# An FNet-gated kernel on one core: earlier draining of four accumulators, one sum taken by an accumulating transfer, and about forty transfers issued by GpSimd instead of SyncE

## The chip, the cores and the metric

One core of a Trainium2 chip runs the whole program. The metric is the device time in microseconds of one execution, the median over several runs. Five engines take part: TensorE (PE in the profile, with its weight loads as PEld), VectorE (DVE), ScalarE (ACT), GpSimd (POOL) and SyncE (SP). SP computes nothing here; it issues transfers. GpSimd computes nothing here either but for a few constants at the start; it too issues transfers.

## What is computed

With S = 2048 tokens and D = 512 features, F = 1792:

```
xn = layernorm(x)
a, b = xn @ Wd_re.T, xn @ Wd_im.T
s = Ws_re @ a - Ws_im @ b                  # FNet mixing, real part
h = relu(xn @ w1 + b1) ** 2
g = silu(h @ w2 + b2)
out = x + s * g
```

Everything is float32.

## The kernel before

A float32 operand is split into a rounded high part (HI, a ScalarE copy, line 138) and the remainder (LO, a VectorE subtraction, line 141). A product then takes three passes on TensorE: HI·HI, HI·LO, LO·HI. Big products are done on 2x2 blocks with seven block products instead of eight, so that operands are needed not only as they are but also as sums of their blocks.

The sequence transform comes first. The tokens lie in eight "x pairs" j (block j and block j + 8, 128 tokens each), the matrix of the transform in eight chunks c of 256 columns. `XC[j]` (tiles `xc`) holds the split operands of pair j, `u` the raw block (c, j) of the transform's matrix with its sums behind it (four quarters raw, four quarters sums), `g` the split form of that. The work comes in this order:

1. A loop over j = 0..7 loads x, normalizes it, splits it and does chunk 0 with plain products (`products`, line 406) into four PSUM banks `accs`.
2. Two steps `plain_step(j)` for j = 4 and 5 (`MIXED`) do chunk 1 of these pairs with eight plain products, 48 matmuls each (line 395). They need neither the sums of x nor those of the matrix.
3. The list `steps`: first (1, 0), (1, 1), (1, 2), (1, 3), (1, 6), (1, 7), then (c, j) for c = 2 to 7. Each step n does seven products of 6 matmuls, 42 in all (line 395), behind a pipeline written out by hand: in iteration n the block of step n + 4 is loaded (`step_load`), the sums of step n + 2 are made (`step_sums`) and step n + 1 is split (`step_split`). The end of a chunk goes out to DRAM as P and Q (`PQD`). In between, `EARLY` makes the second-stage weights: load (`weight`, line 445), sums, split, store to DRAM (line 458), and loads of the stored ones (`load_wd`, line 509).
4. The hidden transform (Y units), the first dense layer (H units) and the second with the gate and the output follow.

What the change touches lies at the seam of 1, 2 and 3:

- `sums(g)` makes the sums of x for four pairs (g = 0: pairs 0 to 3, g = 1: pairs 4 to 7) as a generator: three VectorE subtractions (line 275), one at each `next`, and then four accumulating transfers that GpSimd issues (line 278), 128 KB each, one for each pair. `split_sums(j)` splits what comes out: HI on ScalarE, LO on VectorE.
- `sums_b` makes the four sums of a block of the matrix with three VectorE operations: line 305 writes quarters 4 and 5 (quarter 0 plus quarters 1 and 2), lines 307 and 308 write quarters 6 and 7 out of these.
- `plain_out(k)` copies the four banks of chunk 0 to SBUF on ScalarE (line 148, tiles `plain`), whence SP stores them (line 628).

Each engine carries out its instructions in the order in which the program issues them; a wait of one holds all behind it. Transfers are queued by the engine that issues them. In this kernel SP issues nearly all loads and stores, ScalarE the stores of y and h, and GpSimd the eight accumulating transfers of the sums of x and seven accumulating additions of x near the end (line 945).

Of the kernel before, what the change touches and what calls it, by code (L numbers as in the profile page):

```python
# [8 lines left out]
F32 = mybir.dt.float32  # L9
F32R = mybir.dt.float32r  # L10
AF = mybir.ActivationFunctionType
ALU = mybir.AluOpType

P = 128
S, D, F = 2048, 512, 1792
NS, ND, NF = S // P, D // P, F // P
# [116 lines left out]
def fnet_gated_kernel(ctx, tc, x, xt, ct, wd, w1, w2, b1, b2, out):  # L133
    nc = tc.nc
# [8 lines left out]
    def split(*parts):  # L143
        split_hi(*parts)
        split_lo(*parts)
# [15 lines left out]
    PQD = [dram.tile([P, 2, 4, 256], F32, name=f"pqd{c}") for c in range(NC)]  # L161
    WDD = [dram.tile([P, 2, 7, 256], F32, name=f"wdd{n}") for n in range(ND)]
# [9 lines left out]
    def buf(tag, shape, name, dtype=F32):  # L172
        return pool.tile(shape, dtype, tag=tag, bufs=3 if tag == "u" else 1, name=name)
# [96 lines left out]
    def sums(g):  # L270


        s = xn32[ND * g, "tile"].rearrange("p j h (b n) -> p j (h b) n", b=2)
        for to, a, b in ((3, 1, 3), (1, 1, 0), (0, 3, 0)):
            nc.vector.tensor_tensor(s[:, :, to], s[:, :, a], s[:, :, b], op=ALU.subtract)
            yield
        for j in (1, 0, 3, 2):
            nc.gpsimd.dma_start(s[:, j, 2], s[:, j, 0], accum_op=ALU.add)
        yield

    def split_sums(j):
        s = xn32[j].rearrange("p h (b n) -> p (h b) n", b=2)
        split(XC[j][:, S2:S1 + 1, HI, :], XC[j][:, S2:S1 + 1, LO, :], s)

    raw, part = {}, {}

    def load_c(c, j, hs=slice(0, 2)):
        if (c, j) not in raw:
            raw[c, j] = buf("u", [P, 8, CW], f"u{c}_{j}")
        q = slice(2 * hs.start, 2 * hs.stop)  # L290
        nc.sync.dma_start(raw[c, j][:, q], ct[c, j, :, q])
# [8 lines left out]
    def sums_b(t, r):  # L300
        list(sums_b_steps(t, r))

    def sums_b_steps(t, r):

        nc.vector.tensor_tensor(t[:, 0:2], r[:, 0:1].to_broadcast([P, 2, 256]), r[:, 1:3], op=ALU.add)  # L305
        yield
        nc.vector.tensor_tensor(t[:, 2], t[:, 1], r[:, 1], op=ALU.add)  # L307
        nc.vector.tensor_tensor(t[:, 3], t[:, 2], r[:, 3], op=ALU.add)

# [32 lines left out]
    def step_sums(n):  # L342
        if n < len(steps):
            u = raw[steps[n]]
            sums_b(u[:, 4:8], u)

    def step_split(n):
        if n < len(steps):
            s = steps[n]
            u = raw.pop(s)  # L350
            g = part[s] = buf("g" + "ab"[s[1] % 2], [P, 2, 7, CW], f"g{s[0]}_{s[1]}", F32R)
            split(g[:, HI], g[:, LO], u[:, 1:8])
# [75 lines left out]
    steps = [(1, j) for j in SEVEN] + [(c, j) for c in range(2, NC) for j in range(NJ)]  # L428
    order = [(0, j) for j in range(NJ)] + [(1, j) for j in MIXED] + steps
# [12 lines left out]
    def weight(n, raw_, sums_, to, k, turn=False):  # L442

        r = buf("pq00", [P, 4, 256], f"{n}r")
        nc.sync.dma_start(r, raw_)
        yield
        t = buf("pq01", [P, 4, 256], f"{n}t")
        if turn:
            copy(r[:, I22:I21 + 1], r[:, I22:I21 + 1], -1.0)
        first = sums_(t, r)  # L450
        next(first)
        yield
        list(first)
        yield
        g = buf(f"wd{int(k)}", [P, 2, 7, 256], f"{n}g", F32R)
        for q, src in ((slice(0, 3), r[:, 1:4]), (slice(3, 7), t)):
            split(g[:, HI, q], g[:, LO, q], src)
            nc.sync.dma_start(to[:, :, q], g[:, :, q].bitcast(F32))
            yield

    makers["d"] = lambda n: weight(f"wd{n}", wd[n], sums_b_steps, WDD[n], n % 2, True)
# [43 lines left out]
    def load_wd(n):  # L505
        t = operand_buf(("wd0", "wd1", "xc2", "xc1")[n], f"wdp{n}", 0)
        WDP[n] = t
        for i in range(2):
            nc.sync.dma_start(t[:, i].bitcast(F32), WDD[n][:, i])
            yield  # L510

    makers["y"] = y_early
# [42 lines left out]
    g = plain_parts(0, 1)  # L555
# [3 lines left out]
    def some(steps_, n):  # L559
        for _ in range(n):  # L560
            next(steps_)

    side = sums(0), sums(1)
    load_c(0, 3)
    load_x(4)
    for j in range(1, NJ):
        ln_rstd(j)
        if j == 1:
            ln_hi(j, 0)
            ln_shift(j)  # L570
            ln_xn_act(j, 0)
            ln_mean(j + 1, 1)
            split_lo(*plain_parts(0, j, one))
            ln_xn(j, 1)
            split_hi(*xc_parts(j, 1))
            split_lo(*xc_parts(j, 0))
            split_lo(*plain_parts(0, j, two))
        else:
            if j == NJ - 1:
                ln_shift(j)  # L580
                next(side[0])
            for h in range(2):
                (ln_xn_act if j == NJ - 1 else ln_xn)(j, h)
                split_hi(*xc_parts(j, h))
            split_lo(*g)
            split_lo(*xc_parts(j, 0))
        load_c(*order[j + 3])
        if j in (1, 3, 4):
            load_x({1: 5, 3: 6, 4: 7}[j])
        if j + 1 < NJ:  # L590
            ln_stats(j + 1)
            if j > 1:
                ln_mean(j + 1, 1)
            ln_var(j + 1, 1)
            ln_root(j + 1)
        split_lo(*xc_parts(j, 1))
        if j == NJ - 1:
            some(side[0], 3)
        for h in range(2):
            products(j, h)  # L600
        g = plain_parts(*order[j + 1])
        split_hi(*g)
        if j == 2:
            nc.sync.dma_start(b1s, b1)
            nc.sync.dma_start(b2s, bcast(b2, D))
    split_lo(*g)
    some(side[1], 1)
    step_sums(0)


# [3 lines left out]
    def plain_out(k):  # L614
        to = plain[k // 2].rearrange("p (i m d t) -> p d m i t", i=2, m=2, d=2)[:, k % 2]
        copy(to, accs[k].rearrange("p (m i t) -> p m i t", m=2, i=2))

    for i, j in enumerate(MIXED):
        if i == 0:
            some(side[1], 1)  # L620
            split(*plain_parts(1, MIXED[1]))
            step_sums(1)
            for k in (0, 1):
                split_sums(k)
                plain_out(2 * k)
                plain_out(2 * k + 1)
            for k in range(2):
                nc.sync.dma_start(PQD[0][:, k].rearrange("p k n -> p (k n)"), plain[k])
        else:
            some(side[1], 2)  # L630
            step_split(0)
            split_sums(2)
        plain_step(j)
        load_c(*order[NJ + i + 4])
# [3 lines left out]
    for n, s in enumerate(steps):  # L638
        c, j = s
        if c > 1 and j == 0:  # L640
            ms = {}
        for k, tag in banks(c).items():
            if k not in ms:
                ms[k] = bank(tag, f"m{k}_{c}")
        g = part.pop(s)
        for p in FIRST if j == 0 and c > 1 else ORDER:
            a, b = PRODUCTS[p]
            mm(ms[p], XC[j][:, a], lambda b_: g[:, b_, b], (c > 1 and j == 0) or (not n and p in (1, 5, 6, 7)), s in LAST)
        step_sums(n + 2)
        step_split(n + 1)  # L650
        if n in SUMS_AT:
            split_sums(SUMS_AT[n])
        if n == 0:
            e = buf("e", [P, 2048], "c1")
            copy(chunk_part(e)(C22), halves(ms[Z]))
        step_load(n + 4)
        if closing:
            some(closing, (LATER_1 if c == 2 else LATER).get(j, 0))
            if j in (3, 4):
                q = slice((j - 3) * 1024, (j - 2) * 1024)  # L660
                nc.sync.dma_start(PQD[c - 1][:, j - 3].rearrange("p k n -> p (k n)"), e[:, q])
            if j == 4:
                closing = None
        if s in LAST:
            if c > 1:
                e = buf("e", [P, 2048], f"c{c}")
            room = {}
            if c < NC - 1:
                room = buf("pq10", [P, 2, 512], f"left{c}")
                room = {7: room[:, 0], 5: room[:, 1], 3: buf("pq11", [P, 512], f"left3_{c}")}  # L670
            closing = closing_of(chunk_part(e), ms, room, c == 1)
            some(closing, 2)
        if s == (2, 4):
            nc.vector.transpose(stats_t, stats.rearrange("p m h j -> p (m h j)"))
            for q in range(4):
                nc.sync.dma_start(rows[:, q * 32:(q + 1) * 32], stats_t[q * 32:(q + 1) * 32, :])
        go(*EARLY.get(s, ()))
# [326 lines left out]
    for u in range(2, NC):  # L1004
        n = 2 * u + 2
# [83 lines left out]
    for n in range(NTC * NP):  # L1089
        c, p = divmod(n, NP)  # L1090
# [37 lines left out]
        if p == NP - 1 and not last:  # L1128
            e = buf("e", [P, 4, 512], f"z{c}")
# [16 lines left out]
    e = buf("u", [P, 4, 512], f"z{c}")  # L1146
# [95 lines left out]
```

## Time and profile before

| | |
|---|---|
| median of three runs | 671.6 us (670.96 to 672.92) |
| the profiled execution's own time | 671.6 us |
| its span, first to last instruction | 669.7 us |
| granted TensorE clock, mean | 0.999 |
| PE busy | 662.0 us, 99% |
| DVE busy | 609.6 us, 91% |
| ACT busy | 384.2 us, 57% |
| POOL busy (transfers issued) | 15.9 us, 2% |
| transfers of q1 (issued by SP) | 129.28 MB, 57.9% of 16 DMA engines |
| transfers of q0 (issued by GpSimd) | 2.88 MB, 3.0% |

The profiled execution's time is 1.9 us above its span, and equal to the median of the runs, so that microseconds of the trace can be added to that median. PE is idle for 669.7 - 662.0 = 7.7 us in all. In rows of the trace a name like `g`, `u` or `xc` stands for all tiles of that name, so neighbours in time have to be told apart by their place in the order of the program.

### The profile page before, as it was taken

How to read it: one execution, taken by the hardware profiler on the slowest of the kernel's cores; microseconds unless marked ns; L12 is line 12 of the kernel's file. 1: busy time of each engine (PE TensorE's matmuls, PEld its weight loads, DVE VectorE, ACT ScalarE, POOL GpSimd, SP SyncE). 2: the span in 40 equal slices, each digit the busy share in tenths (PEclk: the TensorE clock that was granted, in tenths of full speed). 3: DMA queues.
4: the chain of work that ended last, by engine and by line, in shares of the span. 5: the costliest groups of instructions: out<-in, count | busy, mean ns of one | idle time of the engine just before them, and what ended most of it. 6: DMA issues, size and time to landing. Idle time of an engine off the chain costs nothing.

```text
span 669.7 us, 13552 instructions
## 1 busy us (share of the span) xinstructions
PE 662.0 (99%) x5593; PEld 650.2 (97%) x5593; DVE 609.6 (91%) x847; ACT 384.2 (57%) x518; POOL 15.9 (2%) x19
## 2 busy tenths in 40 slices
PE   8999999999999999999999999999999999999997
PEld 5889999999999999999999999999999999999997
DVE  7998999899999999999899978977877889999997
ACT  6866554645545454444465457788778865454451
POOL 0013000000000000000000000000000000101010
PEclk9999999999999999999999999999999999999999
DMA  8637535778497785879588557675755866777675
GB/s 285 233 98 185 165 121 169 257 237 253 175 317 241 256 288 175 305 256 342 180 312 266 183 183 294 221 270 192 285 172 204 334 234 203 191 220 200 210 206 156
DMA packets 53756, 151.88 MB, mean 227 GB/s; under 512 B 5184, under 2 KB 20800, under 8 KB 53056
## 3 DMA queue, kind: packets, MB, share of 16 engines
q1 hardware_dynamic: 44432, 129.28, 57.9%
q10 hardware_dynamic: 6208, 18.88, 7.1%
q0 software_dynamic: 3056, 2.88, 3.0%
q8 instruction: 43, 0.70, 0.4%
q14 instruction: 17, 0.14, 0.1%
HBM read 101.98 MB, written 47.99 MB: 224 GB/s over the span
## 4 chain that ended last, share of the span: by engine, by line
PE 89%; DVE 7%; DMA 2%; issue 1%; ACT 1%; SPq 0%; DVEq 0%; ACTq 0%
PE m L395 34%; PE m_o L907 15%; PE r_B L801 13%; PE r_A L801 9%; PE pq_b L406 5%; PE r_C L801 4%; PE r_D L801 4%; PE m_last L907 4%; DVE g L141 2%; PE pq_bb L406 2%; DMA u<-in_ct 1%; DMA x<-in_x 1%; DVE c L380 1%; DVE u L305 1%; ACT g L138 0%
## 5 line engine op out<-in xcount | busy, mean ns | idle before, releaser
L395 PEld LDWEIGHTS m<-g,xc 128*128 128x128 f32 x2364 | 268.5, 188 | 1.9 <-DVE g L141 1.7
L395 PE MATMUL m<-g,xc 128*128 128x256 f32 x2364 | 269.3, 276 | 1.1 <-DVE g L141 1.1
L138 ACT ACTIVATE g<-u 128x1792 fp32r<-128x1792 f32 (+2 forms) x65 | 102.8, 1583 | 126.8 <-PE m L395 85.7
L141 DVE TENSOR_TENSOR g<-u,g 128x1792 fp32r<-128x1792 f32 (+2 forms) x66 | 121.6, 1843 | 4.6 <-ACT g L138 4.1
L907 PE MATMUL m_o<-w,g 128*128 128x256 f32 x882 | 100.5, 276 | 0.0
L907 PEld LDWEIGHTS m_o<-w,g 128*128 128x128 f32 x882 | 100.3, 188 | 0.0
L138 ACT ACTIVATE g<-hr 128x1792 fp32r<-128x1792 f32 (+2 forms) x31 | 48.2, 1566 | 39.9 <-DVE hr L322 17.7
L801 PE MATMUL r_B<-xT,w 128*128 128x256 f32 x504 | 66.4, 276 | 0.0
L801 PEld LDWEIGHTS r_B<-xT,w 128*128 128x128 f32 x504 | 61.4, 188 | 0.0
L141 DVE TENSOR_TENSOR g<-hr,g 128x1792 fp32r<-128x1792 f32 (+2 forms) x31 | 56.7, 1838 | 3.0 <-ACT g L138 2.8
L801 PE MATMUL r_A<-xT,w 128*128 128x256 f32 x336 | 43.1, 276 | 0.1
L406 PE MATMUL pq_b<-g,xc 128*128 128x512 f32 x144 | 40.9, 391 | 1.1 <-DVE small L249 1.1
L801 PEld LDWEIGHTS r_A<-xT,w 128*128 128x128 f32 x336 | 40.3, 188 | 0.3 <-DVE xT L141 0.3
L305 DVE TENSOR_TENSOR u<-u 128x512 f32<-128x512 f32 x54 | 37.0, 684 | 2.1 <-DMA u<-in_ct 2.1
L801 PE MATMUL r_B<-wdp,yg 128*128 128x256 f32 x288 | 35.8, 276 | 0.0
L801 PEld LDWEIGHTS r_B<-wdp,yg 128*128 128x128 f32 x288 | 34.1, 188 | 0.0
L406 PEld LDWEIGHTS pq_b<-g,xc 128*128 128x128 f32 x144 | 26.8, 188 | 7.5 <-ACT g L138 1.6
L907 PE MATMUL m_last<-w,g 128*128 128x256 f32 x294 | 33.5, 276 | 0.0
L907 PEld LDWEIGHTS m_last<-w,g 128*128 128x128 f32 x294 | 33.4, 188 | 0.0
L141 DVE TENSOR_TENSOR yg<-yraw,yg 128x1792 fp32r<-128x1792 f32 x13 | 26.2, 2018 | 0.9 <-ACT yg L138 0.9
L138 ACT ACTIVATE yg<-yraw 128x1792 fp32r<-128x1792 f32 x13 | 22.2, 1707 | 5.4 <-DVE yraw L319 4.5
L307 DVE TENSOR_TENSOR u<-u 128x256 f32<-128x256 f32 x54 | 23.0, 425 | 1.9
(186 smaller groups left out, 843.0 us busy)
## 6 DMA issues: line engine op xcount, KB each, us to landing
u<-in_ct SPq DMA_DIRECT2D x63, 512.0 KB, 3.9
hd<-h ACTq DMA_DIRECT2D x28, 512.0 KB, 4.2
hr<-hd SPq DMA_DIRECT2D x28, 512.0 KB, 3.7
wdp<-wdd SPq DMA_DIRECT2D x8, 896.0 KB, 6.3
yraw<-pqd SPq DMA_DIRECT2D x13, 512.0 KB, 5.5
pqd<-c SPq DMA_DIRECT2D x12, 512.0 KB, 6.1
w<-w1d SPq DMA_DIRECT2D x6, 896.0 KB, 8.4
y<-y ACTq DMA_DIRECT2D x8, 512.0 KB, 5.2
```

What stands on the lines that cost most here:

```text
L138: nc.scalar.activation(hi, src, AF.Copy)
L141: nc.vector.tensor_tensor(lo, src, hi.bitcast(F32), op=ALU.subtract)
L305: nc.vector.tensor_tensor(t[:, 0:2], r[:, 0:1].to_broadcast([P, 2, 256]), r[:, 1:3], op=ALU.add)
L307: nc.vector.tensor_tensor(t[:, 2], t[:, 1], r[:, 1], op=ALU.add)
L380: nc.vector.tensor_tensor(part_(to), halves(room.get(m, ms[m])), part_(frm), op=op)
L395: nc.tensor.matmul(ps[:, d], w[:, a_, d * P:(d + 1) * P], halves(mv(b_)), start=first and d == 0 and (a_, b_) == (HI, HI), stop=last and ( ...
L406: nc.tensor.matmul(accs[k], w, part[0, j][:, b_, 2 * h:2 * h + 2], start=j == 0 and h == 0 and (a_, b_) == (HI, HI), stop=j == NJ - 1 and ...
L801: nc.tensor.matmul(self.region(REGION[k]), w, mv, start=i == 0 and k in (1, 7), stop=i == len(ops) - 1, skip_group_check=True)
L907: nc.tensor.matmul(m[:, i * 256:(i + 1) * 256], ready[n][:, a_, H_SLOT[a], i * P:(i + 1) * P], W2[p][:, b_, b], start=p == 0 and i == 0 an ...
```

## The change

Six edits:

1. ScalarE drains all four banks of chunk 0 ahead of the splits of the sums of x; before, two of the four stood behind the first split and two behind the second. The stores of `plain` are issued ahead of the sums of step 1.
2. For the block of step 0, (1, 0), quarters 4 and 5 are no longer made by VectorE (line 305). SP loads quarters 1 and 2 from DRAM a second time, to their place (line 595 of the changed kernel), and GpSimd issues a transfer that adds quarter 0, read twice from DRAM, on top of them (line 596). VectorE keeps lines 307 and 308 for this block, which are lines 311 and 312 there (`sums_b_rest`).
3. The three subtractions of `sums(1)` are issued later: one each in the first plain step, after the sums of step 1, and in the second plain step. Its four accumulating transfers are issued after step 0.
4. The accumulating transfers are issued in the order in which the pairs are used: 0, 1, 2, 3 and 6, 7, 4, 5, where it was 1, 0, 3, 2 and 5, 4, 7, 6.
5. GpSimd, not SP, issues the loads of the raw weights, the stores of the split ones and the loads of `load_wd`.
6. GpSimd, not SP, issues the stores of P and Q of chunks 1 to 6.

```diff
@@ sums
-        for j in (1, 0, 3, 2):
+        for j in ((0, 1, 2, 3), (2, 3, 0, 1))[g]:
             nc.gpsimd.dma_start(s[:, j, 2], s[:, j, 0], accum_op=ALU.add)
@@ sums_b_steps, step_sums
         nc.vector.tensor_tensor(t[:, 0:2], r[:, 0:1].to_broadcast([P, 2, 256]), r[:, 1:3], op=ALU.add)
         yield
+        sums_b_rest(t, r)
+
+    def sums_b_rest(t, r):
+
         nc.vector.tensor_tensor(t[:, 2], t[:, 1], r[:, 1], op=ALU.add)
         nc.vector.tensor_tensor(t[:, 3], t[:, 2], r[:, 3], op=ALU.add)
...
-            sums_b(u[:, 4:8], u)
+            (sums_b if n else sums_b_rest)(u[:, 4:8], u)
@@ weight, load_wd
-        nc.sync.dma_start(r, raw_)
+        nc.gpsimd.dma_start(r, raw_)
...
-            nc.sync.dma_start(to[:, :, q], g[:, :, q].bitcast(F32))
+            nc.gpsimd.dma_start(to[:, :, q], g[:, :, q].bitcast(F32))
...
-            nc.sync.dma_start(t[:, i].bitcast(F32), WDD[n][:, i])
+            nc.gpsimd.dma_start(t[:, i].bitcast(F32), WDD[n][:, i])
@@ the loop over j, and behind it
         load_c(*order[j + 3])
+        if order[j + 3] == steps[0]:
+            a, b = order[j + 3]
+            u = raw[a, b]
+            nc.sync.dma_start(u[:, 4:6], ct[a, b, :, 1:3])
+            nc.gpsimd.dma_start(u[:, 4:6], ct[a, b, :, 0:1].to_broadcast([P, 2, 256]), accum_op=ALU.add)
...
     split_lo(*g)
-    some(side[1], 1)
     step_sums(0)
@@ the plain steps
         if i == 0:
             some(side[1], 1)
             split(*plain_parts(1, MIXED[1]))
-            step_sums(1)
-            for k in (0, 1):
-                split_sums(k)
-                plain_out(2 * k)
-                plain_out(2 * k + 1)
+            for k in range(ND):
+                plain_out(k)
             for k in range(2):
                 nc.sync.dma_start(PQD[0][:, k].rearrange("p k n -> p (k n)"), plain[k])
+            step_sums(1)
+            some(side[1], 1)
+            split_sums(0)
+            split_sums(1)
         else:
-            some(side[1], 2)
             step_split(0)
+            some(side[1], 1)
             split_sums(2)
@@ the steps
+        if n == 0:
+            some(side[1], 1)
...
-                nc.sync.dma_start(PQD[c - 1][:, j - 3].rearrange("p k n -> p (k n)"), e[:, q])
+                nc.gpsimd.dma_start(PQD[c - 1][:, j - 3].rearrange("p k n -> p (k n)"), e[:, q])
```

The order on VectorE from the end of the loop over j to the split of step 1, before. `g1_4` and `g1_5` belong to the plain steps, `g1_0` and `g1_1` to steps 0 and 1; `xn32_4` holds the sums of x for pairs 4 to 7, `xc0` to `xc2` the split ones of pairs 0 to 2.

```order
L141 TENSOR_TENSOR g1_4_553<-u1_4_428,g1_4_553 128x1024
L275 TENSOR_TENSOR xn32_4_374<-xn32_4_374 128x4x256
L305 TENSOR_TENSOR u1_0_520<-u1_0_520 128x512
L307 TENSOR_TENSOR u1_0_520<-u1_0_520 128x256
L308 TENSOR_TENSOR u1_0_520<-u1_0_520 128x256
L275 TENSOR_TENSOR xn32_4_374<-xn32_4_374 128x4x256
L141 TENSOR_TENSOR g1_5_565<-u1_5_473,g1_5_565 128x1024
L305 TENSOR_TENSOR u1_1_560<-u1_1_560 128x512
L307 TENSOR_TENSOR u1_1_560<-u1_1_560 128x256
L308 TENSOR_TENSOR u1_1_560<-u1_1_560 128x256
L141 TENSOR_TENSOR xc0_121<-xn32_0_184,xc0_121 128x4x256
L141 TENSOR_TENSOR xc1_126<-xn32_0_184,xc1_126 128x4x256
```

Behind these came, before, the third subtraction (L275), the split of `g1_0`, that of `xc2`, the sums of `u1_2` and the split of `g1_1`. The same place on VectorE in the changed kernel, from the row behind the split of `g1_4` on:

```order
L311 TENSOR_TENSOR u1_0_520<-u1_0_520 128x256
L312 TENSOR_TENSOR u1_0_520<-u1_0_520 128x256
L275 TENSOR_TENSOR xn32_4_374<-xn32_4_374 128x4x256
L141 TENSOR_TENSOR g1_5_565<-u1_5_473,g1_5_565 128x1024
L305 TENSOR_TENSOR u1_1_560<-u1_1_560 128x512
L311 TENSOR_TENSOR u1_1_560<-u1_1_560 128x256
L312 TENSOR_TENSOR u1_1_560<-u1_1_560 128x256
L275 TENSOR_TENSOR xn32_4_374<-xn32_4_374 128x4x256
L141 TENSOR_TENSOR xc0_121<-xn32_0_184,xc0_121 128x4x256
L141 TENSOR_TENSOR xc1_126<-xn32_0_184,xc1_126 128x4x256
L141 TENSOR_TENSOR g1_0_636<-u1_0_520,g1_0_636 128x1792
L275 TENSOR_TENSOR xn32_4_374<-xn32_4_374 128x4x256
```

Line 305 of `u1_0` is gone, the sums' rest of `u1_0` now stands first in the row, and each subtraction of `xn32_4` has moved back, the third of them behind the split of `g1_0`.

ScalarE at the same place, before, from the split of `g1_5` to that of `g1_0`:

```order
L138 ACTIVATE g1_5_565<-u1_5_473 128x1024
L138 ACTIVATE xc0_121<-xn32_0_184 128x4x256
L148 ACTIVATE plain0_562<-pq0_b21_130 128x2x2x128
L148 ACTIVATE plain0_562<-pq0_b32_131 128x2x2x128
L138 ACTIVATE xc1_126<-xn32_0_184 128x4x256
L148 ACTIVATE plain1_563<-pq0_bb_132 128x2x2x128
L148 ACTIVATE plain1_563<-pq0_b31_133 128x2x2x128
L138 ACTIVATE g1_0_640<-u1_0_520 128x1792
```

And in the changed kernel:

```order
L138 ACTIVATE g1_5_565<-u1_5_473 128x1024
L148 ACTIVATE plain0_562<-pq0_b21_130 128x2x2x128
L148 ACTIVATE plain0_562<-pq0_b32_131 128x2x2x128
L148 ACTIVATE plain1_563<-pq0_bb_132 128x2x2x128
L148 ACTIVATE plain1_563<-pq0_b31_133 128x2x2x128
L138 ACTIVATE xc0_121<-xn32_0_184 128x4x256
L138 ACTIVATE xc1_126<-xn32_0_184 128x4x256
L138 ACTIVATE g1_0_636<-u1_0_520 128x1792
```

The four copies of the banks have moved ahead of both splits of the sums of x.

GpSimd, its first transfers in the changed kernel; before, the row of `xn32_0` was its first, and behind the two rows of `xn32` came only the additions at the end of the program:

```order
L596 DMA u1_0_520<-in_ct 128x2x256
L278 DMA xn32_0_184<-xn32_0_184 128x256 x4
L278 DMA xn32_4_374<-xn32_4_374 128x256 x4
L449 DMA wd0r_858<-in_wd 128x1024
L672 DMA pqd1_76<-c1_750 128x1024
L462 DMA wdd0_83<-wd0g_1240 256x1x768
L449 DMA wd1r_1244<-in_wd 128x1024
L672 DMA pqd1_76<-c1_750 128x1024
```

The transfer that adds to `u1_0` stands ahead of the sums of x, and the transfers of weights, P and Q follow these in GpSimd's queue.

## The prediction

> **What bounds the kernel now.** I read the page first, then the waits of PE, then PE's timeline at the two places where it waits on VectorE, then the chain and the timelines of the other engines there. First the page: its span, PE's row, and the largest group of matmuls.
>
> ```profile
> span 669.7 us, 13552 instructions
> PE 662.0 (99%) x5593; PEld 650.2 (97%) x5593; DVE 609.6 (91%) x847; ACT 384.2 (57%) x518; POOL 15.9 (2%) x19
> L395 PE MATMUL m<-g,xc 128*128 128x256 f32 x2364 | 269.3, 276 | 1.1 <-DVE g L141 1.1
> ```
>
> PE is busy for all but 7.7 us, and its matmuls are not touched by the change: 269.3 us over 2364 is 0.114 us each, 42 of them or 4.8 us a step. So whatever is gained must come out of these 7.7 us. Where they lie, by PE's waits on VectorE for `g`, by the windows of the start and of the end (start and end of the window, its length, busy time of PE), and by PE's timeline:
>
> ```profile
> PE m L395 <- DVE g L141: 1.1, 2, 0.8
> 0.00:8.00 8.00, 5.69 (x14) 2.82 (x15) 3.89 (x14) 2.99 (x6) 0.20 (x4) 1.00 0.70 231
> 655.00:669.70 14.70, 10.53 (x93) 10.33 (x92) 9.81 (x21) 3.32 (x7) 1.20 (x1) 0.96 0.53 149
> 63.70 16.50 PE L395 MATMUL m<-g,xc 128*128 128x256 f32 x143 [0.77 <-DVE g L141]
> 126.21 4.02 PE L395 MATMUL m<-g,xc 128*128 128x256 f32 x33 [0.34 <-DVE g L141]
> ```
>
> The start takes 8.00 - 5.69 = 2.3, the end 14.70 - 10.53 = 4.2, and neither is touched. That leaves 0.77 at 63.70, where step 0 waits for the low half of its block `g1_0`, and 0.34 at 126.21, where step (3, 0) waits for its own: 1.1 us, or 0.17% of the time. I call a difference under 0.3%, 2.0 us, no change, since that is about what a measurement of this kernel can tell. A gain over 0.3% is therefore all but shut out from the start; what is to be weighed is whether a new wait costs more than that.
>
> The chain shows what stands ahead of the two waits:
>
> ```profile
> 51.92 7.10 PE m L395 x63
> 59.02 0.97 ACT plain L148 x2
> 115.61 6.97 DMA u<-in_ct
> ```
>
> At the first, ScalarE still copies banks of chunk 0 at 59, and only then splits `g1_0`. At the second, a load of the matrix takes 6.97 us.
>
> **Part 1: the banks first.** All four copies now follow the split of `g1_5` on ScalarE, which ends at 53.0 (row below), and the banks have been complete since 51.9. They take some 2 us, twice the 0.97 of the chain's row, in a stretch where ScalarE stood idle until 56.05. After that ScalarE has, ahead of the split of `g1_0`, only the splits of `xc0` and `xc1`. By itself this removes the 0.77.
>
> ```profile
> 51.96 1.06 ACT L138 ACTIVATE g<-u 128x1024 fp32r<-128x1024 f32 x1 [4.54 <-PE pq_b L406]
> 56.05 1.06 ACT L138 ACTIVATE xc<-xn 128x1024 fp32r<-128x1024 f32 x1 [3.02 <-DMA xn<-xn]
> 59.87 1.72 ACT L138 ACTIVATE g<-u 128x1792 fp32r<-128x1792 f32 x1
> ```
>
> **Part 2: two quarters by transfer.** VectorE loses one operation of 0.69 us (line 305 of `u1_0`), and gets a wait in its place: line 311 now stands right behind the split of `g1_4` and needs the accumulating transfer. VectorE is in order, so everything behind it waits too: the split of `g1_5`, the sums of `u1_1`, the splits of `xc0`, `xc1`, `g1_0`, `g1_1`. When does that transfer land? Its forerunner on SP is issued behind the load of `u1_0` (44.14), so at about 44.6. The second row below is the landing of the loads of `u` between 30 and 70 us; the third and fourth are GpSimd's first transfer and its landing (alone); then the landing of the eight accumulating transfers of 128 KB, and of the seven of 256 KB at the end of the program, which have the size and the 1 KB runs from DRAM of the new one.
>
> ```profile
> 44.14 5.21 SPq L291 DMA_DIRECT2D u<-in_ct  x2
> DMA to landing us min/median/max: 3.4/3.7/5.2
> 48.48 2.82 POOL L278 DMA_DIRECT2D xn<-xn  x3 [48.04 <-DVE xn L275]
> DMA to landing us min/median/max: 5.7/5.7/5.7
> DMA to landing us min/median/max: 2.7/5.9/6.8
> DMA to landing us min/median/max: 4.2/4.6/7.0
> ```
>
> The forerunner lands at 44.6 + 3.7 = 48.3. GpSimd's first transfer in the trace begins 0.6 us after VectorE's subtraction that it waits for ends (46.63 + 1.22 = 47.85, below), so the new one begins at about 48.9, while the load of `u1_1` (49.0) is under way, as it was beside the 5.7. Between the median of its own size, 4.6, and that of its own place, 5.7 to 5.9, I take 5.3: it lands at T = 54.2. The ends are 48.9 + 2.7 = 51.6 and 48.9 + 7.0 = 55.9.
>
> The Trainium skill (DMA: Bandwidth & Descriptors, section Anatomy of one DMA, SWDGE path) fits such a transfer as 2.0 us and its bytes at 436 GB/s, an estimate of 2.6 us here, so T = 51.5; none of the rows of that size is so short.
>
> Now VectorE's row, with the durations as it had them:
>
> ```profile
> 46.63 1.22 DVE L275 TENSOR_TENSOR xn<-xn 128x1024 f32<-128x1024 f32 x1
> 47.77 1.22 DVE L141 TENSOR_TENSOR g<-u,g 128x1024 fp32r<-128x1024 f32 x1
> 48.91 1.22 DVE L275 TENSOR_TENSOR xn<-xn 128x1024 f32<-128x1024 f32 x1
> 50.04 0.69 DVE L305 TENSOR_TENSOR u<-u 128x512 f32<-128x512 f32 x1
> 50.76 0.42 DVE L307 TENSOR_TENSOR u<-u 128x256 f32<-128x256 f32 x1
> 51.56 1.22 DVE L275 TENSOR_TENSOR xn<-xn 128x1024 f32<-128x1024 f32 x1
> 53.06 1.23 DVE L141 TENSOR_TENSOR g<-u,g 128x1024 fp32r<-128x1024 f32 x1 [0.28 <-ACT g L138]
> 57.14 1.23 DVE L141 TENSOR_TENSOR xc<-xn,xc 128x1024 fp32r<-128x1024 f32 x1 [1.34 <-ACT xc L138]
> 59.06 1.23 DVE L141 TENSOR_TENSOR xc<-xn,xc 128x1024 fp32r<-128x1024 f32 x1 [0.69 <-ACT xc L138]
> 61.62 2.02 DVE L141 TENSOR_TENSOR g<-u,g 128x1792 fp32r<-128x1792 f32 x1 [0.20 <-ACT g L138]
> 63.57 1.22 DVE L141 TENSOR_TENSOR xc<-xn,xc 128x1024 fp32r<-128x1024 f32 x1
> 66.28 2.02 DVE L141 TENSOR_TENSOR g<-u,g 128x1792 fp32r<-128x1792 f32 x1
> ```
>
> From start to next start, a subtraction or a split of 1024 takes 1.14 us, the three sums of a block 51.56 - 50.04 = 1.52, the last two of them 51.56 - 50.76 = 0.80, a split of 1792 takes 63.57 - 61.62 = 1.95. In the new order, counted from T: the rest of the sums 0.80, the subtraction 1.94, the split of `g1_5` until 3.2, the sums of `u1_1` 4.60, the subtraction 5.74, `xc0` 6.88, `xc1` 8.02, and the split of `g1_0` from there to 8.02 + 2.02 = 10.04; then the third subtraction (which stood ahead of `g1_0` before) 11.1, `xc2` 12.25, the sums of `u1_2` 13.77, and the split of `g1_1` ends at T + 15.8. With T = 54.2:
>
> - `g1_5` is ready at 57.4; PE needs it after 48 matmuls, 51.92 + 5.5 = 57.4. No cost.
> - `g1_0` is ready at 64.2, against 61.62 + 2.02 = 63.64 before: PE's first wait grows by 0.6 instead of going.
> - `g1_1` is ready at 70.0, against 68.3 before, where PE needed it at 63.70 + 4.8 = 68.5. PE loses 70.0 - 68.5 = 1.5 us against before, the 0.6 included.
>
> So a stall of 48.99 to 54.2, 5.2 us, takes the place of the four waits of 0.28, 1.34, 0.69 and 0.20 in these rows, 2.5 us, and of the 0.69 of line 305. After this the split of a step comes every 1.14 + 1.52 + 1.95 = 4.6 us against PE's 4.8, so nothing more is lost and nothing is made up. **Term: +1.5 us**; per microsecond of T one microsecond, zero at T = 52.7, never below -0.77.
>
> **Part 3: later sums of pairs 4 to 7.** Their transfers began here:
>
> ```profile
> 62.05 2.63 POOL L278 DMA_DIRECT2D xn<-xn  x3 [6.69 <-ACT g L138]
> ```
>
> They move to about T + 11.1 + 0.6 = 66. The first user is the split of `xc6`, pair 6 being first in the queue now: landing 5.9 later, at 72, and ScalarE's half of 1.06 make it ready at 73, and VectorE comes to it behind `g1_2`, at 70.0 + 4.6 = 74.6. Hidden, with 1.6 us to spare; a microsecond more than that would be one on VectorE.
>
> **Part 4: the queue of SP.** Here are the issues ahead of the slow load, who waited for it, and ScalarE there:
>
> ```profile
> 111.29 0.33 SPq L661 DMA_DIRECT2D pqd<-c  x1
> 112.16 0.60 SPq L458 DMA_DIRECT2D wdd<-wd0g  x1
> 112.81 0.63 SPq L445 DMA_DIRECT2D wd1r<-in_wd  x1
> 122.61 0.69 DVE L305 TENSOR_TENSOR u<-u 128x512 f32<-128x512 f32 x1 [1.39 <-DMA u<-in_ct]
> 122.69 0.61 ACT L148 ACTIVATE wd1r<-wd1r 128x512 f32<-128x512 f32 x1
> 125.84 1.70 ACT L138 ACTIVATE g<-u 128x1792 fp32r<-128x1792 f32 x1 [2.54 <-PE m L395]
> ```
>
> The load at 115.61 stands behind these three in its own queue, and VectorE stood 1.39 us for it. With those in GpSimd's queue the load has its own; if it takes 5.2 (the slowest of the row above) instead of 6.97, the 1.39 and so PE's 0.34 are gone. The bounds are -0.34 and 0. The Trainium skill bears on both: the same page's section Queues, rings and completion order lets each DMA engine take turns between queues, by packets, and the section Issuing engines are not separate DMA queues holds that spreading issues saves only the issue time. By the second the term would be 0 and the forecast 0.3 us higher. I take **-0.34**: the bytes stay, but not the order. The new cover is thin at one place, `wd1r`: ScalarE used it at 122.69 and then stood idle for 2.54 us, so it may land that much later on GpSimd's queue without cost. No other change of issuer has PE behind it in the trace.
>
> **Sum:** 671.6 + 1.5 - 0.3 = **672.8 us**, made against the profiled execution, whose own time is the median.
>
> **The rivals.**
>
> *A, the forecast* (55 in 100): VectorE's stall replaces the old ones; T from 53 to 55 gives 671.6 to 673.6.
>
> *B, the gain arrives* (20): the accumulating transfer lands by 51.6, as the fastest row had it; then `g1_1` is ready at 67.4, no wait is left, and 671.6 - 0.77 - 0.34 = 670.5. Against it: only the last of a batch took 2.7, with nothing beside it. The fit of the Trainium skill above would have it so.
>
> *C, slower* (20): the queue of GpSimd. The fourth transfer of a batch was held:
>
> ```profile
> 54.48 0.88 POOL L278 DMA_DIRECT2D xn<-xn  x1 [3.18 <-issue]
> ```
>
> It left at 54.48, right after the first had landed (48.48 + 5.7 = 54.2). If GpSimd can have only so much outstanding, the new transfer, twice as large, holds back the sums of pair 1 until T + 0.3. With 5.9 to land they come at T + 6.2, `xc1` is split on ScalarE until T + 7.3, `g1_0` until T + 9.0, and VectorE can begin with it 1.0 later than counted. It decides when pair 1 lands after T + 5.2. With T = 54.8 (5.9) the loss is 2.1 + 1.0, less 0.3: 674.4.
>
> *D, nothing is relieved* (5): transfers of GpSimd carry 1 KB runs at less speed, and a weight or a P or Q lands late somewhere after 126, or the load there stays as slow: 673.1 upward, more if a step waits.
>
> **How the numbers follow.** The likeliest is A, 672.8. B ends at 670.5, C reaches from 673.8 to 675.5 with T at its far end. From 670.6 to 674.9 holds A, most of B and most of C. Faster by over 0.3% would need 2.0 us where 1.1 are to be had: 0.03. Slower by over 0.3%, above 673.6: C, and the edges of A and D: 0.24. The rest, 0.73, is no change.
>
> **What would show it.** Right: in VectorE's waits a new one of about 5 us on line 311, ended by a transfer into `u`; PE's waits on `g` near 64 and 70 adding to about 2.3 us, none at 126; the load there under 6 us. Wrong: no wait at line 311 (B); a wait of ScalarE for `xn` past 60 (C); PE waiting anywhere behind 126 for weights or P and Q (D). If PE's idle total falls to 6.6 us I was wrong on part 2.

## The result and the profile after

The changed kernel takes 678.65 us, median of four runs (678.05 to 680.21), beside 671.28 us for the kernel before in the same comparison (670.4 to 672.92). The ratio is 1.011, with a 95% interval of 1.0083 to 1.0138: slower by 7.4 us, where 1.2 were forecast. The profiled execution took 678.12 us.

The page first: its span, PE's row, the two largest groups that changed, and PE's and VectorE's waits (waited for: us in total, times, the longest).

```profile
span 676.2 us, 13578 instructions
PE 665.0 (98%) x5593; PEld 652.4 (96%) x5593; DVE 608.3 (90%) x846; ACT 384.2 (57%) x518; POOL 41.3 (6%) x61
L305 DVE TENSOR_TENSOR u<-u 128x512 f32<-128x512 f32 x53 | 36.3, 684 | 7.6 <-DMA u<-in_ct 7.6
L311 DVE TENSOR_TENSOR u<-u 128x256 f32<-128x256 f32 x54 | 23.0, 425 | 7.8 <-DMA u<-in_ct 6.0
```

```profile
PE m L399 <- DVE g L141: 4.9, 7, 1.2
DVE u L305 <- DMA u<-in_ct: 7.6, 4, 2.3
DVE u L311 <- DMA u<-in_ct: 6.0, 1, 6.0
```

PE stands idle for 676.2 - 665.0 = 11.2 us, 3.5 more than before, and its waits on `g` have gone from 1.1 to 4.9. The wait at line 311 is the forecast one. The wait at line 305, 7.6 us for loads of `u`, stood at 2.1 before, and the forecast had it shrink. PE is also 3.0 us longer "busy", though it has the same matmuls. Where the waits lie, by PE's timeline (start, length, the wait ahead of it in brackets):

```profile
57.41 0.84 PE L399 MATMUL m<-g,xc 128*128 128x256 f32 x5 [0.71 <-DVE g L141]
64.27 5.22 PE L399 MATMUL m<-g,xc 128*128 128x256 f32 x42 [1.15 <-DVE g L141]
70.00 40.27 PE L399 MATMUL m<-g,xc 128*128 128x256 f32 x348 [0.51 <-DVE g L141]
128.25 1.99 PE L399 MATMUL m<-g,xc 128*128 128x256 f32 x15 [0.29 <-DVE g L141]
220.14 25.26 PE L399 MATMUL m<-g,xc 128*128 128x256 f32 x210 [0.89 <-DVE g L141]
246.03 47.89 PE L399 MATMUL m<-g,xc 128*128 128x256 f32 x420 [0.64 <-DVE g L141]
294.63 5.57 PE L399 MATMUL m<-g,xc 128*128 128x256 f32 x45 [0.71 <-DVE g L141]
```

So there are two separate losses: three waits at the start (2.4 us, against the one of 0.77), and three behind 200 us where before had none (2.2 us). The wait near 126 is still there, 0.29 after 0.34. The rows also show the longer busy time: behind the wait at 220.14, 210 matmuls take 25.26 us, 0.120 each, and behind the one at 246.03, 420 take 47.89, 0.114 each as before. At 0.114 the 210 would take 23.9, so that stretch alone is 1.3 us longer. A part of the 3.0 us comes from how busy time is counted: the last matmul ahead of a wait counts with its full 0.276 us, where otherwise the next one begins after 0.114. That is 0.16 us for each wait, and for five more waits an estimated 0.8 us. The cause of the rest stays open (see the last section).

The second loss, followed back. PE waits at 220.14 for a split; VectorE's timeline of the changed kernel ahead of it:

```profile
216.54 0.69 DVE L305 TENSOR_TENSOR u<-u 128x512 f32<-128x512 f32 x1 [2.21 <-DMA u<-in_ct]
218.06 2.02 DVE L141 TENSOR_TENSOR g<-u,g 128x1792 fp32r<-128x1792 f32 x1
```

And the issues ahead of it, GpSimd's and SP's in the changed kernel:

```profile
206.02 0.70 POOL L462 DMA_DIRECT2D w1d<-w10g  x1 [8.78 <-DVE w10g L141]
206.61 0.68 POOL L449 DMA_DIRECT2D w11r<-in_w  x1
207.26 0.56 POOL L513 DMA_DIRECT2D wdp<-wdd  x1
209.10 0.33 SPq L291 DMA_DIRECT2D u<-in_ct  x1
```

The landing of that one load of `u`, by the view of its tile:

```profile
DMA to landing us min/median/max: 7.4/7.4/7.4
```

SP's issues at the same place before:

```profile
207.67 0.33 SPq L291 DMA_DIRECT2D u<-in_ct  x1
208.22 0.33 SPq L509 DMA_DIRECT2D wdp<-wdd  x1
```

And the landing of that load of `u`:

```profile
DMA to landing us min/median/max: 4.0/4.0/4.0
```

Before, SP's queue was stopped at the load of `u`, which waits for VectorE to free its buffer, and the 0.9 MB of stored weights (`wdp`) stood behind that and went out 0.55 us after it. On GpSimd they don't stand behind that load: they go out 1.84 us ahead of it, and it takes 7.4 us and not 4.0. The median landing of all 63 loads of `u` is 3.9 us on both pages. Four loads are waited for in the changed kernel. The one near 118 took 6.9 us, as it had before (7.0); the loss sits in the other three, which took 7.4, 8.1 and 7.6 us near 209, 234 and 283, where they had taken 4.0, 5.7 and 3.5.

The load near 234 is a case of its own. Here are `wdp` and that load, in the changed kernel and then before:

```profile
231.41 0.53 POOL L513 DMA_DIRECT2D wdp<-wdd  x1
234.31 0.33 SPq L291 DMA_DIRECT2D u<-in_ct  x1
```

```profile
227.36 0.42 SPq L509 DMA_DIRECT2D wdp<-wdd  x1
230.82 0.33 SPq L291 DMA_DIRECT2D u<-in_ct  x1
```

There `wdp` went out ahead of the load before as well, by 3.46 us, and now by 2.90 us on the other queue. So no order was lost at this place.

### The profile page after: what moved, and what is told of

The parts are those of the page before. It is cut to its first block, busy times and chain, and to the rows that moved or that the text cites. A ratio compares the mean times of both kernels' runs of the same rounds, so it can differ in the third digit from the quotient of the medians.

```text
span 676.2 us, 13578 instructions
## 1 busy us (share of the span) xinstructions
PE 665.0 (98%) x5593; PEld 652.4 (96%) x5593; DVE 608.3 (90%) x846; ACT 384.2 (57%) x518; POOL 41.3 (6%) x61
## 4 chain that ended last, share of the span: by engine, by line
PE 73%; DVE 16%; DMA 6%; issue 2%; ACT 1%; SPq 0%; DVEq 0%; ACTq 0%; POOLq 0%
PE m L399 24%; PE m_o L918 15%; PE r_B L812 13%; PE r_A L812 9%; DMA u<-in_ct 6%; DVE g L141 6%; PE r_C L812 4%; PE r_D L812 4%; PE m_last L918 4%; DVE xc L141 2%; DVE u L305 1%; ACT g L138 1%; DVE u L311 1%; DVE xn L275 1%; DVE c L384 1%
## 5 line engine op out<-in xcount | busy, mean ns | idle before, releaser
L399 PE MATMUL m<-g,xc 128*128 128x256 f32 x2364 | 272.6, 277 | 5.0 <-DVE g L141 4.9
L138 ACT ACTIVATE g<-hr 128x1792 fp32r<-128x1792 f32 (+2 forms) x31 | 48.2, 1565 | 39.9 <-PE m_o L918 16.7
L141 DVE TENSOR_TENSOR g<-hr,g 128x1792 fp32r<-128x1792 f32 (+2 forms) x31 | 56.7, 1838 | 3.0 <-ACT g L138 2.8
L956 POOL DMA_DIRECT2D z<-in_x x7 | 8.5, 1213 | 342.1 <-DVE z L968 301.9
```

Of the source, the lines that this page charges most:

```text
L138: nc.scalar.activation(hi, src, AF.Copy)
L141: nc.vector.tensor_tensor(lo, src, hi.bitcast(F32), op=ALU.subtract)
L399: nc.tensor.matmul(ps[:, d], w[:, a_, d * P:(d + 1) * P], halves(mv(b_)), start=first and d == 0 and (a_, b_) == (HI, HI), stop=last and ( ...
L956: nc.gpsimd.dma_start(z, at(x[c * TC:(c + 1) * TC], k), accum_op=ALU.add)
```

## The experiments

**Theory Q**: what costs behind 200 us is the moment of issue. SP's order kept the large transfers behind the loads of `u`; without it they get ahead. **Rival F**: the start leaves VectorE no lead, and the loads hurt only for that. **Rivals S and S2**: it is the second queue, or GpSimd's software queue, whatever the moment (the profile lists GpSimd's queue q0 as software_dynamic, those of SP and ScalarE, q1 and q10, as hardware_dynamic). Microseconds below are the ratio less one, times 671; two expectations quote an earlier result as a difference of medians instead (+7.1 for what is +6.4 here, +4.5 for +5.2).

**The issuers alone** (edits 5 and 6 put on the kernel before):

```diff
-        nc.sync.dma_start(r, raw_)
+        nc.gpsimd.dma_start(r, raw_)
...
-            nc.sync.dma_start(t[:, i].bitcast(F32), WDD[n][:, i])
+            nc.gpsimd.dma_start(t[:, i].bitcast(F32), WDD[n][:, i])
...
```

> Only the issuer of weights, P and Q is changed (edits 5 and 6); the start is that of before. Theory Q: in SP's queue these transfers went out behind loads of u that were waited for, and so were spaced; in GpSimd's queue they go out as soon as their own data stand, ahead of a load of u or two at a time, and the load beside them takes 7 to 8 us instead of 4 to 6. By that this kernel loses what the changed one lost behind 200 us: 3.2 near 220 to 250 and 1.5 near 293 to 309, so +4 to +5 us, with waits of PE on g near 220, 246 and 294 and loads of u of over 7 us near 209, 234 and 283. Rival F: the start leaves VectorE without a lead, and the loads only hurt for that reason; then this kernel is within 1 us of before, though its loads of u are as slow.

675.61 us, ratio 1.0073 (1.0060 to 1.0087): +4.9. The load of `u` at 207.17, 1.84 us behind a `wdp`, took 7.4 us again. PE waits on `g` for 1.23 us at 126 (0.34 before), 0.90 at 218, 1.36 at 244 and 0.19 at 292. Rival F falls: the start is that of before. In this profile the wait near 64 is absent too, though nothing ahead of it was changed; in other versions with the start of before it is 0.77 to 1.39 us. So one profile can't tell a gain or a loss of that size there.

**The start alone** (the changed kernel with the four kinds of transfers back on SP):

```diff
-            nc.gpsimd.dma_start(t[:, i].bitcast(F32), WDD[n][:, i])
+            nc.sync.dma_start(t[:, i].bitcast(F32), WDD[n][:, i])
...
```

> Edits 1 to 4 alone: banks first, two quarters by the accumulating transfer, later sums, order of the pieces; weights, P and Q are issued by SP as before. Theory Q: the loss of the first 100 us stays, from 0.8 ahead to 2.0 behind, and nothing is lost later: +2 to +3 us, a wait of VectorE at line 311 of about 6 us, none of PE on g behind 130. Rival F: most of the whole +7.4 stays. The forecast's part 2 alone would be +1.5.

674.32 us, ratio 1.0052 (1.0039 to 1.0065): +3.5, a little over what was expected. VectorE waits 6.5 us at line 311. PE's waits on `g` at the start (one of 0.16 follows at 209.85):

```profile
58.38 5.72 PE L399 MATMUL m<-g,xc 128*128 128x256 f32 x48 [1.22 <-DVE g L141]
65.24 5.22 PE L399 MATMUL m<-g,xc 128*128 128x256 f32 x42 [1.14 <-DVE g L141]
70.96 2.31 PE L399 MATMUL m<-g,xc 128*128 128x256 f32 x18 [0.51 <-DVE g L141]
```

4.9 + 3.5 = 8.4, within the interval of the whole (5.6 to 9.3): within the noise the two losses add.

**The start without the accumulating transfer** (as above, and VectorE makes all four sums of that block):

```diff
-            u = raw[a, b]
-            nc.sync.dma_start(u[:, 4:6], ct[a, b, :, 1:3])
-            nc.gpsimd.dma_start(u[:, 4:6], ct[a, b, :, 0:1].to_broadcast([P, 2, 256]), accum_op=ALU.add)
...
-            (sums_b if n else sums_b_rest)(u[:, 4:8], u)
+            sums_b(u[:, 4:8], u)
```

> Edits 1, 3 and 4 alone: VectorE makes all four sums of the block of step 0 again (line 305), no accumulating transfer into u, weights, P and Q on SP. If part 1 of the forecast holds, the wait of PE near 64 goes and nothing is put in its place: -0.8 to -1.6 us (0.8 of that because x comes earlier at the start). If the order of the sums of x itself costs something, it is 0 or above.

670.25 us, ratio 0.9993 (0.9981 to 1.0004): -0.5, which can't be told from nothing. In the profile no wait of PE on `g` is left (the last column is the idle time ahead of the group):

```profile
L399 PE MATMUL m<-g,xc 128*128 128x256 f32 x2364 | 268.1, 276 | 0.0
```

So the whole loss of the start comes with edit 2. Its parts are told apart further down.

**Only the loads of the stored weights on GpSimd** (before, with line 509 alone):

```diff
-            nc.sync.dma_start(t[:, i].bitcast(F32), WDD[n][:, i])
+            nc.gpsimd.dma_start(t[:, i].bitcast(F32), WDD[n][:, i])
```

> Before, with only the loads of the stored weights (two of 0.9 MB for each of four) on GpSimd. Theory Q: of the loads of u near 209, 234 and 283, two stand beside these loads; so of the +4 to +5 of the issuers about half or more, +2 to +3 us, with the wait near 294 and that near 220 but not that near 246. Rival: what costs is the sum of all that moved, and this alone is under 1 us.

677.82 us, ratio 1.0096 (1.0082 to 1.0109): +6.4, more than the +2 to +3 expected and more than with all four kinds moved. These eight transfers are enough. With GpSimd's queue otherwise empty they went out still further ahead: here two of them, issued at 202.28 and 202.84, 5.0 and 4.4 us ahead of the load of `u`. GpSimd's row and SP's, and then the landing of the first of the two loads:

```profile
202.28 1.10 POOL L509 DMA_DIRECT2D wdp<-wdd  x2 [134.72 <-DVE g L141]
207.25 4.98 SPq L291 DMA_DIRECT2D u<-in_ct  x2
```

```profile
DMA to landing us min/median/max: 8.6/8.6/8.6
```

PE waits 2.11 us at 219.51, then 0.73 at 311.59 and 0.41 at 317.04. There is none near 246, as expected, but none near 294 either.

**The issuers alone, held** (GpSimd waits once a step for the write that also releases the load of `u`):

```diff
+        if n + 1 < len(steps):
+            nc.gpsimd.tensor_copy(stats_t[:, 0:1], part[steps[n + 1]][:, LO, 6, 0:1].bitcast(F32))
```

> As the kernel with the issuers alone changed, but once a step GpSimd first copies one element per partition of the low half that VectorE writes last for the next step (into stats_t, which is unused then), so that its transfers go out right after the load of u of that step, which waits for the same write. Queue, ring and bytes are those of GpSimd as in the kernel with the issuers alone changed. Theory Q (the moment of issue decides): the loads of u are ahead again; they take 4 to 6 us near 209, 234 and 283, and the loss of +4.9 falls to between 0 and +1.5. Rival S (a second queue, or GpSimd's, takes its share of the engines at any moment of issue): the loss stays at +4 to +6. The 46 copies themselves lie on GpSimd, which computes nothing else.

674.01 us, ratio 1.0035 (1.0021 to 1.0049): +2.3 (1.4 to 3.3), half of the 4.9. GpSimd made 53 of these copies, not 46. GpSimd's rows there, and then the landing of the load of `u` issued at 207.29:

```profile
207.40 0.18 POOL L652 COPY stats_t<-g 128x1 f32<-128x1 f32 x1 [1.94 <-DVE g L141]
208.07 0.54 POOL L509 DMA_DIRECT2D wdp<-wdd  x1 [0.49 <-issue]
```

```profile
DMA to landing us min/median/max: 4.5/4.5/4.5
```

With the same queue and the same bytes, but 0.78 us behind the load, `wdp` costs the load 0.5 us and not 3.4. The load near 283 shows the same: here, at 279.49, it took 3.4 us, where it had taken 7.6 in the changed kernel. PE's waits near 220 and 294 are gone. So for these two loads the moment of issue is shown.

It isn't all. The load at 230.74, the case of its own above, still took 7.2 us, with `wdp` 2.98 us ahead of it on GpSimd; before, with `wdp` 3.46 us ahead in SP's own queue, it took 5.7. That is half a microsecond less lead, and a second queue (rival S). The version below with the stored weights back on SP speaks for the queue: there `wdp` is 4.05 us ahead, only the stores of P and Q stand on GpSimd, and the load takes 6.8. It doesn't settle it, since the store ahead of the load has less lead there as well (3.45 us, before 3.84). Theory Q expected 1.5 at most, which the interval just reaches, and what is left of the 2.3 isn't assigned. Of PE's waits on `g` in this profile, 1.38 us lie at 63.94, ahead of all that the edit touches, and 0.29, 0.41 and 0.25 behind.

**The stored weights on ScalarE's queue**:

```diff
-            nc.sync.dma_start(t[:, i].bitcast(F32), WDD[n][:, i])
+            nc.scalar.dma_start(t[:, i].bitcast(F32), WDD[n][:, i])
```

> Before, with only the loads of the stored weights issued by ScalarE, which has a hardware queue of its own. ScalarE is done with its half of a split some 2 us before VectorE frees the buffer that the load of u of that step waits for. Theory Q: these loads go out ahead of a load of u as on GpSimd, so +3 to +6 with waits of PE near 220 and 310. Rival S2 (it is GpSimd's software queue that costs): within 1 us of before.

675.94 us, ratio 1.0064 (1.0037 to 1.0091): +4.3 (2.5 to 6.1; single runs from 672.26 to 679.67), with a wait of PE of 1.48 us at 310. The one near 220 is only 0.15. The load of `u` at 207.35, 0.70 us behind a `wdp`, took 6.3 us. The one at 298.82, with two `wdp` 4.2 and 3.8 us ahead of it, took 8.0. GpSimd's software queue isn't needed for a loss of this size, and S2 falls.

**The issuers alone, stored weights back on SP**:

```diff
-            nc.gpsimd.dma_start(t[:, i].bitcast(F32), WDD[n][:, i])
+            nc.sync.dma_start(t[:, i].bitcast(F32), WDD[n][:, i])
```

> The issuers alone changed, but the loads of the stored weights back on SP: raw weights, stores of the split ones, P and Q stay on GpSimd. Theory Q: the loads of the stored weights alone cost +7.1, so this costs little, 0 to +2, with at most one wait of PE on g behind 100 us. If the cost goes with the number of transfers on GpSimd (32 of the 40), +4.

672.07 us, ratio 1.0012 (1.0001 to 1.0023): +0.8. The other 33 transfers cost little. Where they cost is near 127: there PE waits 1.46 us in the profiled execution (673.87 us, the longest of eleven), behind a load of `u` that took 8.1 us and not 7.0.

**The sums' rest later** (the start alone, with line 311 behind the split of `g1_5`), against the first loss:

```diff
     split_lo(*g)
-    step_sums(0)
...
             split(*plain_parts(1, MIXED[1]))
+            step_sums(0)
```

> As the kernel with the start alone changed, but VectorE's rest of the sums of step 0 (line 311) stands behind the second subtraction of the sums of x and the split of g1_5, so that VectorE works while the accumulating transfer is under way. If the wait at line 311 is what the start costs (part 2 of the forecast), it falls from 6.5 us to under 1, the waits of PE near 58, 65 and 71 go, and the +3.5 falls to between -1.0 and +0.5, about the kernel with all sums on VectorE (-0.5). If the accumulating transfer costs by something else (ScalarE's wait for the sums of x, held in GpSimd's ring behind it), +1 or more stays.

676.08 us, ratio 1.0077 (1.0060 to 1.0095): +5.2, and so worse, not better. The wait at line 311 fell to 0.4 us, as expected. Another had been behind it. The rows of GpSimd, ScalarE and PE:

```profile
48.17 1.34 POOL L596 DMA_DIRECT2D u<-in_ct  x1 [47.73 <-DMA u<-in_ct]
49.02 1.44 POOL L278 DMA_DIRECT2D xn<-xn  x1
54.15 2.66 POOL L278 DMA_DIRECT2D xn<-xn  x3 [3.69 <-issue]
60.23 1.06 ACT L138 ACTIVATE xc<-xn 128x1024 fp32r<-128x1024 f32 x1 [4.47 <-DMA xn<-xn]
61.20 1.68 ACT L138 ACTIVATE g<-u 128x1792 fp32r<-128x1792 f32 x1
64.99 3.36 PE L399 MATMUL m<-g,xc 128*128 128x256 f32 x17 [1.68 <-DVE g L141]
```

The sums of pairs 1 to 3 are held until the transfer into `u` has landed; pair 1 arrives at 60.2, ScalarE waits 4.47 us for it, and the split of step 0's block stands behind it. That is rival C of the prediction, which the wait at line 311 had covered. PE also waits 1.30 us at 130.08 and 0.47 at 212.18, for reasons that aren't shown. To test the account, **the same without the transfer**; this kernel leaves out a term of the sums of one block:

```diff
-            nc.gpsimd.dma_start(u[:, 4:6], ct[a, b, :, 0:1].to_broadcast([P, 2, 256]), accum_op=ALU.add)
```

> As the kernel with the late rest, but the accumulating transfer into u is left out: quarters 4 and 5 of the block of step 0 hold only what SP loaded, so the sums of that one block lack a term. All else stays, SP's second load of two quarters too. Theory R: with the wait at line 311 out of the way, the +4.5 of the late rest came from GpSimd's ring: the sums of x of pairs 1 to 3 were issued only when the transfer into u had landed (at 54.15), pair 1 landed at 60.2, and ScalarE waited 4.5 us for it ahead of the split of the block of step 0. Without the transfer they are issued near 49, pair 1 lands near 55, ScalarE's wait for xn is under 1 us, PE's waits near 63 and 65 go, and the time is -1.5 to +0.5 against before. Rival: the late place of the sums or SP's second load is the cause; then +2 or more stays.

670.89 us, ratio 0.9998 (0.9983 to 1.0013). GpSimd's and ScalarE's rows:

```profile
47.99 2.82 POOL L278 DMA_DIRECT2D xn<-xn  x3 [47.54 <-DVE xn L275]
54.32 2.03 ACT L138 ACTIVATE xc<-xn 128x1024 fp32r<-128x1024 f32 x2
56.94 1.71 ACT L138 ACTIVATE g<-u 128x1792 fp32r<-128x1792 f32 x1 [0.60 <-ACT xc L138]
```

The first three sums go out at once, ScalarE waits for none, and no wait of PE on `g` is left. The late place and SP's second load of two quarters cost nothing that can be told; GpSimd's transfer does, by the wait at line 311 or, once that is out of the way, by the three sums held behind it.

**The changed kernel with the two undone** (all four sums on VectorE, stored weights on SP):

```diff
-            nc.gpsimd.dma_start(t[:, i].bitcast(F32), WDD[n][:, i])
+            nc.sync.dma_start(t[:, i].bitcast(F32), WDD[n][:, i])
...
-            nc.gpsimd.dma_start(u[:, 4:6], ct[a, b, :, 0:1].to_broadcast([P, 2, 256]), accum_op=ALU.add)
...
-            (sums_b if n else sums_b_rest)(u[:, 4:8], u)
+            sums_b(u[:, 4:8], u)
```

> The changed kernel with two things undone: VectorE makes all four sums of the block of step 0, and the loads of the stored weights are on SP again. Raw weights, stores of the split ones, P and Q stay on GpSimd, the banks first, the order of the sums as changed. If these two carry the whole loss, the rest adds up to -0.5 (the start without the transfer) + 0.8 (issuers without the stored weights): 0 to +1 against before, out of +7.4. If they act together with something else in the change, +2 or more stays.

671.05 us, ratio 0.9998 (0.9986 to 1.0011). The two carry the whole loss, the longer busy time of PE included: it is 661.0 us here, after 665.0 in the changed kernel. PE still waits 1.3 us on `g`, at 124.63 and 240.11. No version here beats the kernel before by more than the measurement can tell.

**The price of a wait of PE** (the start without the transfer, sums of three blocks repeated):

```diff
-        step_sums(n + 2)
+        for _ in range(1 + {6: 2, 16: 3, 24: 4}.get(n, 0)):
+            step_sums(n + 2)
```

> The start without the transfer and all on SP (-0.5, no wait of PE on g behind 50 us), with the three sums of one block done three, four and five times over on VectorE (same result) in steps 6, 16 and 24: 3.0, 4.6 and 6.1 us more on VectorE each time. It asks for the price of a wait of PE. In the changed kernel the matmuls behind some waits of PE came every 117.7 ns, and not every 113.3, for up to 22 us at a granted clock of 1.00. Theory W: a wait brings such a stretch with it, so PE's busy time rises by 0.3 to 0.9 us for each wait, over the 661.4 us without. Rival: the stretches have another cause (the transfers beside them); then PE's busy time stays within 0.3 us of 661.4, and the loss is the waits alone, 0 to 9 us by VectorE's lead.

689.21 us, ratio 1.0247 (1.0215 to 1.0279): +16.6, more than either expectation (four runs, 684.04 to 689.37). The waits behind the three delays are 1.97, 3.41 and 5.21 us long, 10.6 together, but PE's busy time rose from 661.4 to 668.9 as well. Four of the windows around the first of them (start and end, length, PE, PEld, DVE, ACT, POOL busy; granted clock; DMA share; GB/s):

```profile
96.00:97.00 1.00, 0.00 (x0) 0.00 (x0) 1.00 (x1) 1.00 (x1) 0.00 (x0) 1.00 0.03 8
98.00:99.00 1.00, 1.00 (x9) 1.00 (x9) 1.00 (x3) 0.00 (x0) 0.00 (x0) 0.86 0.23 33
99.00:100.00 1.00, 1.00 (x7) 1.00 (x6) 0.93 (x3) 0.00 (x0) 0.00 (x0) 0.50 0.75 287
102.00:103.00 1.00, 1.00 (x10) 1.00 (x9) 1.00 (x3) 0.00 (x0) 0.00 (x0) 0.93 0.02 4
```

The clock is granted at half for about three microseconds, beginning one behind the end of a wait of 2 us. Around the third wait, of 5.21 us, it was granted at 0.57 from 194 to 196, while PE was still waiting. Neither of the two theories had this, so the run doesn't decide between them. And it isn't what slowed the changed kernel, whose granted clock is 1.00 in its slow stretches.

## Why the prediction was wrong, point by point

- **The bound** held: no more than 1.1 us was there to be had, and the start without the transfer, with no wait on `g` left, came to -0.5, which can't be told from nothing.
- **Part 1** held as far as it can be told. The wait of 0.77 is gone where nothing takes its place. But no run has edit 1 alone, and the issuers alone, with the banks as before, had no wait there either.
- **Part 2** had the mechanism right and the size too small. The term that was mis-sized is the landing of the transfer: forecast 5.3 us, measured 6.0, and 6.5 in the start alone. That it landed at 54.2, the T of the forecast, is luck. The whole start ran 0.7 to 0.8 us earlier than in the profile of before: VectorE came to line 311 at 48.2 and not 48.99, the transfer was issued at 48.16 and not 48.9, and PE wanted `g1_5` at 56.7 and not 57.4. Measured against PE, the transfer was 0.7 us late, which by the forecast's rule of one for one makes +2.2. So "`g1_5` ... No cost" failed: it was ready at 57.4, and the wait is 0.71 (1.22 in the start alone). The forecast set the two at 57.4 and 57.4, with no margin, and charged nothing for it. The waits near 64 and 70 add to 1.7 where 2.3 were forecast. "After this nothing more is lost" failed too: PE's 42 matmuls behind the wait at 64.27 took 5.22 us, where a step had taken 4.8. The term was +1.5 and measured +3.5.
- **Part 3** held: the transfers began at 65.95, where 66 was forecast, and no later sum of x was waited for.
- **Part 4** is the step that failed, worst in the sentence "No other change of issuer has PE behind it in the trace". Each moved transfer was asked only when it would land itself; it was not asked which load it had been standing behind in SP's queue. The rows were there: in the trace of before, `wdp` at 208.22 directly behind `u` at 207.67. What the runs showed in its place: two loads of `u`, near 209 and 283, were overtaken by the `wdp` that they had kept back, and took 7.4 and 7.6 us where they had taken 4.0 and 3.5; a third, near 234, was slower (8.1 us, not 5.7) without being overtaken, which the second queue may explain, but that stays open. The term of -0.34 failed as well: "with those in GpSimd's queue the load has its own" was no relief. That load took 6.97 us before and 6.9 after, and 7.9 and 8.1 with the issuers alone and with all but the stored weights moved, where PE waited 1.23 and 1.46 us and not 0.34. The term measured +4.9. Of the Trainium skill's page DMA: Bandwidth & Descriptors, the section Queues, rings and completion order lets each DMA engine take turns between queues by packets. The traces fit that, though they don't show the turns: a load issued 1.84 us behind another queue's 0.9 MB took 7.4 us where it took 4.0 ahead of it. The section Issuing engines are not separate DMA queues, by which spreading saves only issue time, gives 0. That is nearer than -0.34, but here the loss of the order cost more than the issue time could save.
- **The rivals**: D came nearest and had 5 in 100. Its clause that the load near 126 "stays as slow" came true, but for the rest it watched for late weights and late P and Q, and it was the matrix that came late. C's mechanism is real, as the late rest shows, but did not decide: in the changed kernel the three sums were held until 54.43 too, and ScalarE's longest wait for them, 2.03 us, ended at 58.13, before the 60 that was to be its sign.

## What to carry to other kernels

A queue that is issued in order is also a schedule: a transfer that stands behind a waiting one is kept out of its way, here 0.55 us behind the load instead of 1.84 us ahead of it. Before transfers are moved to an idle issuer, list for each what it stands behind and how much lead that has; the cost is paid by what stays. And a median landing time says nothing about the few loads that have no lead: it was 3.9 us in both kernels. Last, look at each slow load by itself: the one near 234 had not been overtaken, and holding the issues back did not mend it.

## What the runs showed of the hardware that was not expected

- GpSimd's accumulating transfers: with one of 256 KB and one of 128 KB under way, the next of 128 KB was held from 50.5 to 54.15, 0.3 us after the first had landed (48.17 + 5.7, in the late rest). Of four of 128 KB before, three went out at once and the fourth 3.18 us later. That the landing releases the next one fits these times. Without the transfer into `u`, three of the sums went out at once, as shown above.
- PE has stretches in which the same matmuls come 4 to 5% slower at a granted clock of 1.00 and without a wait between them. They follow some waits, but one stands in the late rest without the transfer, which has no wait on `g` ahead of it. Its windows, in the stretch and behind it:

```profile
66.00:82.00 16.00, 15.97 (x136) 15.77 (x135) 15.71 (x17) 7.95 (x6) 0.88 (x1) 1.00 0.54 152
82.00:98.00 16.00, 16.00 (x143) 16.00 (x142) 15.36 (x21) 10.30 (x10) 0.00 (x0) 1.00 0.38 125
```

  There are 136 matmuls in a time that holds 143. In the changed kernel the stretch behind 220 makes up 1.3 of the 3.0 us of longer busy time. What causes them stays open.
- A wait of PE of 1.97 us was followed by half the granted clock for some 3 us; one of 2.11 us, in the kernel with only the stored weights moved, was followed by a clock of 1.00. What tells them apart stays open.
